# Warm-up matmuls that read a constant of the preamble, begun without VectorE, and two more of them

## Chip, cores, metric

One core of a Trainium2 chip. The metric is device microseconds of the whole kernel, the median over runs.

## The reference

The output mixes two branches of the same input x of 2048 tokens by 1024, both gated by a sigmoid. Branch a, a diagonal complex state-space model with 1024 states, is nearly all of the work at the start:

```python
g = sigmoid((x * gate_w).sum(-1, keepdims=True))
Bu = einsum("bld,pd->blp", x, B_bar)          # real and imaginary planes
h  = Lam_bar * h + Bu[:, t, :]                # scan over t
a  = 2.0 * einsum("blp,dp->bld", hseq, Cmat).real + x * Dskip
b  = x + scatter(moe(x[top 8 tokens]))
out = g * a + (1 - g) * b
```

## The kernel before

What the change and the argument touch is the first 24 us. The sync queue issues, one behind the other, the transposing loads of B (two planes, eight blocks) and of x; PE warms its clock with 14 matmuls on a zeroed tile, transposes the first 256 rows of x, which are loaded plainly, and starts on B.

```python
for tl in range(BPC):                                   # x rows 0..255, plain loads
    (nc.scalar if tl else nc.sync).dma_start(x0r[:, tl, :], x2d[tl * P:(tl + 1) * P, :])
load_B(0, 0, 1)                                         # transposing loads on the sync queue
...
new_X(0)
load_xT(1)                                              # x rows 256..511, transposing load
load_B(1, 0, 1)
for c0, c1 in ((1, 2), (2, 3), (3, 4), (4, 6), (6, 8)):
    for pl in range(2):
        load_B(pl, c0, c1)
...
wt0 = small.tile([P, LC], BF16, name="wt0", tag="wt")
nc.vector.memset(wt0[:], 0.0)
...
def warm(n):
    for _ in range(n):
        nc.tensor.matmul(wps[:], lhsT=wt0[:, 0:P], rhs=wt0[:], start=True, stop=True)

warm(14)
for tl in range(BPC):
    xq = ps_s2.tile([P, KD, P], BF16, name="xq", tag="zps")
    for dc in range(KD):
        nc.tensor.transpose(xq[:, dc, :], x0r[:, tl, dc * P:(dc + 1) * P], ident[:])
    ...                                                 # VectorE and ScalarE copy xq into X[0]
warm(2)
...
warm(1)
s1u(0, 0, 0, 0, 1)       # 8 matmuls, block 0 of B, real plane, first half of x
warm(2)
s1u(0, 0, 0, 1, 2)       # second half
s1u(0, 0, 1, 0, 2)       # imaginary plane
...
M["xsel32"] = small.tile([P, KD, 32], BF16, name="xsel32", tag="wt")   # reuses wt0's buffer
nc.gpsimd.memset(M["xsel32"][:], 0.0)
```

The results of the warm-ups are read by nobody.

## Time and profile before

| | |
|---|---|
| median, 3 runs | 247.49 us (247.28 to 247.5) |
| profiled execution | 247.9 us, span 246.1 us |
| first warm-up | 1.07 us |
| x0r lands, transposes begin | 4.11 us |
| PE's last wait for a load of B ends | 23.61 us |
| PE's last matmul ends | 242.95 us |

The lines of the profile stand in the prediction. Read them in this order: the chain, to see who sets the end in which stretch; the waits of PE; then the timeline of the stretch that the change touches. In a line of the timeline the columns are start, length of the group, engine, line, operation, names and shapes, count, and in brackets the idle time before it with its releaser. A group's length is from its first start to its last end, and the end of a matmul is modelled, so step times are worked out from starts.

### The profile page before, as it was taken

The numbers are of one execution on the slowest core, as the hardware profiler recorded it, in microseconds if no ns is written. First come the engines' busy times: TensorE is split into PE (matmuls) and PEld (weight loads), VectorE is DVE, ScalarE is ACT, GpSimd is POOL, SyncE is SP. The second block draws the span as 40 slices with busy tenths as digits, with TensorE's granted clock in tenths as the row PEclk, the third lists the DMA queues.
The fourth block names the chain that finished last, engine by engine and source line by source line (L and its number), as shares of the span: only waits on it lengthen the run. The fifth ranks groups of instructions, "written<-read, shape, count | busy, mean of one in ns | idle before, by whom it ended". The sixth has DMA issues, their size and how long they took to land.

```text
span 246.1 us, 3533 instructions
## 1 busy us (share of the span) xinstructions
PE 240.6 (98%) x1381; PEld 112.2 (46%) x1381; DVE 226.2 (92%) x230; ACT 119.3 (48%) x206; POOL 26.8 (11%) x47
## 2 busy tenths in 40 slices
PE   8998999999999999999999999999999999999994
PEld 5443444444444444444444444444444444446453
DVE  1799999999999999999999999999999999999932
ACT  3699973333462572223355462235267445456421
POOL 4000000000000301620002040100100211110210
PEclk9999999999999999999999999999999999999999
DMA  7899999999760450666257979778599999962052
GB/s 195 194 149 226 230 244 273 202 239 284 236 181 0 106 153 0 134 125 224 77 188 218 351 226 338 237 224 314 184 390 286 363 306 296 89 142 37 3 133 82
DMA packets 65313, 48.48 MB, mean 197 GB/s; under 512 B 50560, under 2 KB 52224, under 8 KB 65296
## 3 DMA queue, kind: packets, MB, share of 16 engines
q1 hardware_dynamic: 59968, 37.20, 58.1%
q0 software_dynamic: 3264, 7.38, 14.3%
q10 hardware_dynamic: 2064, 3.68, 4.1%
q8 instruction: 11, 0.18, 0.3%
q14 instruction: 6, 0.05, 0.1%
HBM read 27.55 MB, written 8.40 MB: 146 GB/s over the span
## 4 chain that ended last, share of the span: by engine, by line
PE 89%; SPq 7%; DMA 2%; issue 0%; DVE 0%
PE zps L767 42%; PE vps L271 39%; SPq L80 6%; PE zps L783 3%; PE pgu L659 3%; DMA BT<-in_A_B_im_dram 2%; PE y L671 1%; SPq L92 1%; PE zr L485 1%; DVE ot L788 0%; SPq L77 0%; PE xselT_ps L572 0%; PE zs_ps L588 0%; PE zt L492 0%; PE fl_ps L535 0%
## 5 line engine op out<-in xcount | busy, mean ns | idle before, releaser
L271 PE MATMUL vps<-X,BT 128*128 128x512 bf16 (+1 forms) x520 | 112.6, 376 | 1.2 <-DMA BT<-in_A_B_im_dram 0.9
L767 PE MATMUL zps<-CT,H 128*128 128x512 bf16 x480 | 105.0, 379 | 0.0
L271 PEld LDWEIGHTS <-BT 128*128 128x128 bf16 x520 | 50.1, 98 | 61.7 <-DMA BT<-in_A_B_im_dram 1.7
L767 PEld LDWEIGHTS <-H 128*128 128x128 bf16 x480 | 46.5, 98 | 56.6 <-issue 1.3
L278 ACT CAST V<-vps 128x512 bf16<-128x512 f32 x64 | 34.3, 588 | 58.6 <-PE vps L271 58.6
L308 DVE TENSOR_TENSOR_SCAN U<-d,U 128x2048 bf16<-128x2048 f32 (+2 forms) x22 | 62.0, 2860 | 0.6
L772 ACT ACTIVATE ot<-zps,gcol 128x512 bf16<-128x512 f32 x30 | 20.6, 686 | 46.3 <-PE zps L767 46.3
L741 ACT CAST zps<-xd 128x512 f32<-128x512 bf16 (+1 forms) x29 | 16.6, 576 | 3.6 <-ACT xt L728 3.3
L297 DVE TENSOR_TENSOR U<-V,T2tab 128x4096 bf16<-128x4096 bf16 (+2 forms) x11 | 16.6, 1511 | 0.7 <-ACT V L278 0.2
L298 DVE TENSOR_TENSOR V<-V,nTi 128x4096 bf16<-128x4096 bf16 (+2 forms) x11 | 16.7, 1516 | 0.5
L299 DVE TENSOR_TENSOR U<-U,V 128x4096 bf16<-128x4096 bf16 (+2 forms) x11 | 16.7, 1516 | 0.4
L793 POOL DMA_DIRECT2D out_dram<-ot x14 | 12.9, 923 | 32.5 <-ACT ot L772 30.4
L333 DVE TENSOR_TENSOR U<-U,S2tab 128x4096 bf16<-128x4096 bf16 x7 | 16.0, 2292 | 0.2
L335 DVE TENSOR_TENSOR H<-H,U 128x4096 bf16<-128x4096 bf16 x7 | 16.0, 2292 | 0.2
L728 ACT ACTIVATE xt<-xt,omgcol 128x1024 bf16<-128x1024 bf16 x14 | 16.0, 1144 | 0.0
L331 DVE TENSOR_TENSOR H<-U,Ctab 128x4096 bf16<-128x4096 bf16 x7 | 16.0, 2284 | 0.0
L705 POOL DMA_DIRECT2D xt<-in_A_x_dram x12 | 7.1, 594 | 80.9 <-DMA out_dram<-xt 42.9
L366 DVE TENSOR_TENSOR_SCAN U<-D,U 128x1024 bf16<-128x1024 f32 x4 | 8.9, 2279 | 0.1
L723 DVE TENSOR_TENSOR xd<-xt,Dbc 128x1024 bf16<-128x1024 bf16 x14 | 9.0, 683 | 0.0
L659 PE MATMUL pgu<-wgu,xsel 128*32 128x448 bf16 x128 | 7.2, 355 | 0.0
L783 PE MATMUL zps<-CT,H 128*128 128x256 bf16 (+1 forms) x48 | 7.1, 308 | 0.0
L718 POOL DMA_DIRECT2D out_dram<-xt x2 | 1.5, 752 | 49.2 <-DVE xt L717 49.2
(152 smaller groups left out, 127.6 us busy)
## 6 DMA issues: line engine op xcount, KB each, us to landing
wgu<-in_B_w_gate_dram SPq DMA_DIRECT2D x16, 448.0 KB, 3.5
wgu<-in_B_w_up_dram SPq DMA_DIRECT2D x16, 448.0 KB, 6.1
out_dram<-ot POOLq DMA_DIRECT2D x14, 256.0 KB, 6.0
wdb<-in_B_w_down_dram SPq DMA_DIRECT2D x7, 512.0 KB, 10.6
xt<-in_A_x_dram POOLq DMA_DIRECT2D x12, 256.0 KB, 4.3
out_dram<-xt ACTq DMA_DIRECT2D x12, 256.0 KB, 5.2
wd<-in_B_w_down_dram SPq DMA_DIRECT2D x5, 512.0 KB, 7.8
xt<-in_A_x_dram SPq DMA_DIRECT2D x4, 256.0 KB, 4.1
```

Of the source, the lines that this page charges most:

```text
L271: nc.tensor.matmul(o, lhsT=BT[pl][:, dc, ct * P:(ct + 1) * P], rhs=X[m][:, dc, k0 * LC:k1 * LC], start=(dc == 0), stop=(dc == KD - 1))
L278: nc.scalar.copy(out=V[k][:, :, ct, :], in_=vp[m, ct][:, :, kk, :])
L297: nc.vector.tensor_tensor(out=u, in0=v, in1=T2tab[:, :, c0:c1, :], op=ALU.mult)
L298: nc.vector.tensor_tensor(out=v, in0=v, in1=bc(nTi, c0, c1), op=ALU.mult)
L299: nc.vector.tensor_tensor(out=u, in0=u, in1=V[k][:, ::-1, c0:c1, :], op=ALU.add)
L308: nc.vector.tensor_tensor_scan(out=fl, data0=d0[:, c0:c1, :].rearrange("p c t -> p (c t)"), data1=fl, initial=0.0, op0=ALU.mult, op1=ALU.add)
L331: nc.vector.tensor_tensor(out=h, in0=g, in1=bc(Ctab, c0, c1), op=ALU.mult)
L333: nc.vector.tensor_tensor(out=g, in0=g, in1=S2tab[:, :, c0:c1, :], op=ALU.mult)
L335: nc.vector.tensor_tensor(out=h, in0=h, in1=G[k][:, ::-1, c0:c1, :], op=ALU.add)
L741: nc.scalar.copy(out=z[:], in_=xd[b][:, d_:d_ + w])
L767: nc.tensor.matmul(zps[:], lhsT=H[k][:, pl, ct, tl * P:(tl + 1) * P], rhs=CT[pl][:, ct, dsl], start=(fresh and ct == 0 and pl == 0), stop= ...
L772: nc.scalar.activation(out=ots[b][:, dsl], in_=zps[:], func=ACT.Copy, scale=gcol[:, b:b + 1])
```

## The change

The intent is to start the warm-ups without waiting for VectorE. They now read a constant of ones that the preamble writes before the barrier: one element per partition, read with a step of 0 as a 128x256 operand. Two more fill the time gained.

```diff
-    wt0 = small.tile([P, LC], BF16, name="wt0", tag="wt")
-    nc.vector.memset(wt0[:], 0.0)
+    wt0 = nc.const_aps.tensor(1.0, [P, LC], BF16)
...
-            nc.tensor.matmul(wps[:], lhsT=wt0[:, 0:P], rhs=wt0[:], start=True, stop=True)
-
-    warm(14)
+            nc.tensor.matmul(wps[:], lhsT=wt0[:, 0:P], rhs=wt0, start=True, stop=True)
+
+    warm(16)
```

## The prediction

> **What bounds the kernel now.** I read the page first (busy time, slices, chain), then the chain in order of time, then the waits of PE, then the timeline of the first microseconds, and last the busy time of chosen stretches.
>
> ```profile
> span 246.1 us, 3533 instructions
> PE 240.6 (98%) x1381; PEld 112.2 (46%) x1381; DVE 226.2 (92%) x230; ACT 119.3 (48%) x206; POOL 26.8 (11%) x47
> PE 89%; SPq 7%; DMA 2%; issue 0%; DVE 0%
> ```
>
> PE is busy 240.6 of 246.1 us, so idle 5.5 us in all. The chain that sets the end lies on PE for 89%, but 7% and 2% are the sync queue and a DMA. Where those 9% lie matters, since the change touches only the start. The chain in order of time:
>
> ```profile
> 0.74 0.39 SPq L77
> 1.20 1.32 SPq L80
> 2.57 2.60 SPq L92
> 5.21 1.31 SPq L80
> ...
> 14.68 3.56 SPq L80
> 18.24 0.04 issue
> 18.29 5.27 DMA BT<-in_A_B_im_dram
> 23.56 0.05 issue
> 23.61 36.43 PE vps L271 x168
> ```
>
> The first 23.6 us of the chain are not PE at all. They are a queue of transposing loads of B and x issued one behind the other by SP, each some 1.3 us or more, and the landing of a block of B_im at 23.56. PE takes the chain at 23.61 and keeps it. The waits of PE over the whole execution agree:
>
> ```profile
> PE wps L152 <- DVE halfpi L132: 1.1, 1, 1.1
> PE vps L271 <- DMA BT<-in_A_B_im_dram: 0.9, 2, 0.7
> PE vps L271 <- DMA X<-in_A_x_dram: 0.2, 1, 0.2
> ```
>
> PE waits 1.1 us for VectorE at the very start (the wait that the change takes away), and later 1.1 us for DMAs, of which 0.7 us is the wait that ends at 23.61. Then nothing. The busy times of four stretches (columns: stretch and length, then busy us and starts of PE, PEld, DVE, ACT, POOL, granted clock, DMA share, GB/s):
>
> ```profile
> 1.06:3.86 2.80, 2.79 (x14) 1.95 (x14) 0.00 (x0) 1.28 (x1) 2.17 (x7) 1.00 0.73 213
> 4.11:5.00 0.89, 0.89 (x17) 0.89 (x17) 0.23 (x1) 0.00 (x0) 0.00 (x0) 1.00 1.22 259
> 22.90:23.61 0.71, 0.00 (x1) 0.01 (x1) 0.71 (x3) 0.71 (x2) 0.00 (x0) 1.00 0.62 81
> 23.61:242.95 219.34, 219.30 (x1261) 101.02 (x1261) 208.91 (x181) 101.86 (x173) 23.61 (x32) 1.00 0.75 200
> ```
>
> From 23.61 to 242.95 PE is busy 219.30 of 219.34 us. Just before, from 22.90, it stands still for 0.71 us. So anything that PE does before 22.9 us is separated from the end by an idle stretch that a DMA ends. And the start itself:
>
> ```profile
> 0.84 0.17 DVE L129 MEMSET wt<- 128x128 uint32 x1 [0.84 <-PEq L932]
> 1.06 2.69 PEld L152 LDWEIGHTS <-wt 128*128 128x128 bf16 x14 [1.06 <-DVE halfpi L132]
> 1.07 3.06 PE L152 MATMUL wps<-wt 128*128 128x256 bf16 x14 [1.07 <-DVE halfpi L132]
> 4.11 0.90 PEld L159 LDWEIGHTS <-x0r 128*128 128x128 bf16 x16 [0.35 <-DMA x0r<-in_A_x_dram]
> 4.11 1.07 PE L159 MATMUL xq<-ident,x0r 128*128 128x128 bf16 x16
> 7.26 0.32 POOL L505 MEMSET xsel<- 128x256 bf16 x1 [4.04 <-PE wps L152]
> ```
>
> The 14 warm-ups begin at 1.07, after the memset (0.84 + 0.17 = 1.01, plus some 0.05 for the semaphore). Fourteen start within 1.06 to 3.86, the last about 3.86, so 13 steps in 2.79 us: 0.215 us each. The first useful work, the 16 transposes of x, begins at 4.11 because the load of x0r lands then, not because of the warm-ups.
>
> **What the Trainium skill says.** "TensorE: Matmul & The Clock Gate", Part 1, says that PE starts throttled at 1.2 GHz and goes to 2.4 GHz after some 3.4 us of sustained activity, seen through a window that runs freely and doesn't reset with the kernel; the gap of matmuls is N/1.2 ns cold and N/2.4 + 2.5 ns warm. For N = 256 that is 213 and 109 ns. The trace agrees: 215 ns a step for the warm-ups, while 17 starts (16 transposes of 128 columns and one warm-up) fit in 0.89 us from 4.11, or 52 ns each against the page's 56. So the switch came between about 3.86 and 4.11, some 2.8 to 3.05 us after PE's first matmul. (The granted clock of 1.00 in every stretch doesn't show this switch; the steps do.) "VectorE: DVE Perf Modes", section on zero memsets as uint32, says that a zero memset over 16-bit elements may run as uint32 at half the elements; the trace agrees: the 128x256 bf16 tile is written as 128x128 uint32 in 0.17 us. So what is removed was already cheap. The "FWL" row of the clock page's weight-path section allows column steps from -1,023 to 1,024, which includes the step 0 of the new operand; no run of before shows a step of 0.
>
> **The change part by part.**
> 1. The memset of wt goes: one VectorE instruction, 0.17 us at 0.84. VectorE has nothing else until the copy of X at 4.77 (it waits 3.75 us for PE there), so nothing on it moves: gain 0.
> 2. The first warm-up waits only for the start barrier. Other engines leave it at 0.74 (SP, POOL), 0.75 (ACT) and 0.84 (VectorE). I put PE's first matmul at 0.85, choosing the late end, so 1.07 - 0.85 = 0.22 us earlier.
> 3. Two more warm-ups at 0.215 cold: +0.43 us of PE, or +0.22 if both are warm (109 ns). If all 16 are cold the last step ends at 0.85 + 16 x 0.215 = 4.29. If the clock switches at about 3.95 as before, some 14.4 are done cold by then and the other 1.6 take 0.17: end about 4.12. If the switch moves with the start, to 3.73, 13.4 are done and 2.6 take 0.28: end about 4.01.
> 4. So the transposes begin at 4.11 to 4.29, against 4.11: between 0 and +0.18 us on PE there, and the first copies of X as much later. PE's slack behind: it waits 0.24 us for B_re at 5.93, 0.24 for x at 7.44, 0.18 for B_im at 8.65, and 0.71 before 23.61. The last two alone are 0.89 us. A delay of 0.18 disappears in the first of them; a gain disappears just as well, because the DMAs decide.
> 5. The sync queue: its transposing loads up to 23 us wait for earlier DMAs, and none for PE. The loads begin after the barrier at 0.74 and don't move: 0. The comparison of the two orders shows the sync and scalar queues with the same instructions and waits.
> 6. The clear of xsel on POOL reused the buffer of wt and waited 4.04 us for the last warm-up. In the new order it waits for nothing, so it goes after POOL's last DMA issue (2.66 + 0.56 = 3.22) instead of 7.26. POOL's next work is at 14.17: 0.
> 7. Four more PE rows (two weight loads, two matmuls), 0.43 us more busy time for PE, in a stretch before the bound begins.
>
> Sum on the path that sets the end: 0 + 0 + 0 = 0. Median 247.4 us, the 247.49 of before less a tenth for nothing but rounding: I expect no change.
>
> **The rivals.**
> (a) The earlier start is a real gain of 0.2 us, or more, because the clock switches earlier. For it: the authors evidently meant it, and 1.1 us is the longest wait of PE in the list. Against it: the transposes before are already at 52 ns a step, so warm when they begin, and x0r lands at 4.11 whatever PE does. It could pay only in executions in which the free window switches late (up to the page's 3.4 us later, half of it lost: 1.7 us, an estimate from the page, of which 0.9 us or more is absorbed). The three times, 247.28 to 247.5, show no such scatter. At best 246.7.
> (b) The two extra warm-ups replace the wait by work and delay the transposes by 0.18 us. For it: 16 x 0.215 = 3.44 us is longer than 4.11 - 0.85 = 3.26. Against it mattering: the 0.71 us idle before 23.61. It makes 247.5. Nothing of it reaches the end unless the scalar or vector work that hangs on X passes it on; after 23.61 PE shows no wait for them.
> (c) Reading one element over and over (step 0) is slower for PE. If each cold warm-up took twice as long, 16 x 0.43 = 6.9 us would end at 7.7, 3.6 us late; less the slack of 0.24 + 0.24 + 0.18 + 0.71 = 1.4 us, the end would come some 2.2 us later: 249.7. Still within 2%. Nothing in the trace speaks for or against; I give it 4%.
>
> **Range and chances.** The core is 0 +/- 0.2 us from the parts, the scatter of before is 0.22 us over three runs, and another chip or session may shift both by a few tenths. Range 246.9 to 247.9. To be faster by 2% would take 4.9 us, and PE's whole idle time is 5.5 us with 3.15 of it behind the last matmul: below 1%. Slower by 2% needs more than rival (c) gives: 1%. Within 2%: 98.5%.
>
> **What would show it right or wrong.** Right: the first warm-up at 0.75 to 0.9 waiting for no VectorE; 16 warm-ups with steps near 215 ns; transposes at 4.1 to 4.3; the clear of xsel near 3.2; the same SP issues at the same times; the DMA wait before 23.6 still there, shorter or longer by at most 0.2 us; PE from there to the end unchanged at about 219.3 us. Wrong: warm-up steps well above 215 ns, transposes beyond 5 us, or a wait before 23.6 that has vanished while PE begins that stretch later; a vanished wait together with an earlier landing of B_im would mean a gain that I don't see.

## The result

| | median | range | runs |
|---|---|---|---|
| before | 247.50 us | 247.19 to 247.58 | 6 |
| changed | 247.63 us | 247.31 to 248.19 | 6 |

The ratio is 1.0009, with a 95% interval of 0.9994 to 1.0024: no difference. Ratios in this document are the mean time of one kernel's runs over the mean of the other's runs of the same rounds. This one uses all six runs of each; those of the experiments come out, within 0.0002, when the first run of each list, the profiled one, is left out. So they are not quite the ratios of the medians quoted, which include it. Executions over 1.5% slower than the fastest of the same kernel are left out of the means.

The page of the changed kernel (span, and the chain by engine):

```profile
span 245.6 us, 3535 instructions
PE 98%; DVE 0%; issue 0%
```

The chain in order of time:

```profile
0.78 3.57 PE wps L151 x16
4.35 1.73 PE xq L158 x16
...
10.76 48.70 PE vps L270 x224
```

The timeline of the start and the only wait of PE in the whole execution:

```profile
0.78 3.57 PE L151 MATMUL wps<-const-bfloat16-1.0 128*128 128x256 bf16 x16 [0.78 <-PEq L931]
3.21 0.33 POOL L504 MEMSET xsel<- 128x256 bf16 x1
4.18 1.62 PEld L158 LDWEIGHTS <-x0r 128*128 128x128 bf16 x16 [0.32 <-DMA x0r<-in_A_x_dram]
4.19 1.89 PE L158 MATMUL xq<-ident,x0r 128*128 128x128 bf16 x16
10.69 48.77 PE L270 MATMUL vps<-X,BT 128*128 128x512 bf16 x224
```
```profile
PE wps L151 <- PEq L931: 0.8, 1, 0.8
```

And the stretch that holds the last 1261 starts of PE (columns as in the prediction):

```profile
23.20:242.41 219.21, 219.13 (x1261) 100.96 (x1259) 209.95 (x185) 102.77 (x175) 23.62 (x32) 1.00 0.76 199
```

Three things are to be seen. The start did what was intended: 0.78 instead of 1.07, and PE no longer waits for VectorE. But the first weight load of the transposes still waits 0.32 us, for the load of x, until 4.18, where before it waited 0.35 us until 4.11: what PE does first of use begins no earlier. Two things differ from before that the edit doesn't explain at once. First, the 16 transposes take 1.89 us from first start to last end where before they took 1.07: they ran at half rate, so the clock switched only near 6 us, not near 4. Second, the DMA waits of PE are gone, and the chain now lies on PE from 0.78 us on: 98% instead of 89%. PE does the rest in the same time as before (219.13 us for 1261 starts, against 219.30). So this one execution had a later clock, earlier loads, and a span 0.5 us shorter, while the medians say that nothing changed. Both oddities needed a test: are they the change, or chance?

### The profile page after: what moved, and what is told of

Its sections match the earlier page's. It is cut to its first block, busy times and chain, and to the rows that moved or that the text cites. A ratio compares the mean times of both kernels' runs of the same rounds, so it can differ in the third digit from the quotient of the medians.

```text
span 245.6 us, 3535 instructions
## 1 busy us (share of the span) xinstructions
PE 241.5 (98%) x1383; PEld 113.4 (46%) x1383; DVE 225.8 (92%) x229; ACT 119.1 (49%) x206; POOL 26.8 (11%) x47
## 4 chain that ended last, share of the span: by engine, by line
PE 98%; DVE 0%; issue 0%
PE vps L270 45%; PE zps L766 42%; PE zps L782 3%; PE pgu L658 3%; PE wps L151 2%; PE y L670 1%; PE zr L484 1%; PE xq L158 1%; DVE ot L787 0%; PE xselT_ps L571 0%; PE zs_ps L587 0%; PE zt L491 0%; PE va_ps L165 0%; PE vb_ps L435 0%; PE fl_ps L534 0%
```

## The experiments

The theories. W: the clock's window runs freely, so the moment of the switch varies from execution to execution in both kernels, and PE has enough slack ahead of the B loads to hide it. O: the new operand wakes the clock later. S: the slack is about 1 us, and what exceeds it costs time one for one. N: the start of PE doesn't matter at all. All comparisons are with the kernel before in the same rounds (11 or 12 runs of it, 6 of each experiment).

### The two kernels again

No edit. The kernel before:

> The kernel before, unchanged, for a second profile and to see the scatter. Theory W (the clock's window runs freely, so the switch falls anywhere, whatever the operand): ratio 1.000 within 0.15%, and the 16 transposes of x may now be cold (1.7 us) as well as warm (0.9 us). Theory O (the new operand, ones read with a step of 0, wakes the clock later than zeros in memory do): the transposes are warm again, about 0.9 us from first start to last. On the load of B: PE's DMA wait near 23.6 us is 0.7 us if that is a habit, anything from 0 to 0.7 if it is the scatter of the transposing loads.

Measured: 247.75 us median (247.31 to 249.01), ratio 1.0009 (0.9984 to 1.0034). The kernel before against itself gives the very ratio of the change: this is what noise looks like here. Its timeline:

```profile
1.07 3.17 PE L152 MATMUL wps<-wt 128*128 128x256 bf16 x14 [1.07 <-DVE halfpi L132]
4.27 1.85 PE L159 MATMUL xq<-ident,x0r 128*128 128x128 bf16 x16
```

Zeros in memory, 14 warm-ups, and the transposes are cold all the same. The changed kernel:

> The changed kernel, unchanged, for a second profile. Theory W: ratio 1.000 to 1.001, transposes warm or cold by chance. Theory O: transposes cold again (1.7 us), the switch near 6 us. If the change costs something steady of its own, the ratio stays above 1.001 with an interval that leaves 1 out.

Measured: 247.48 us median (247.19 to 249.07), ratio 0.9994 (0.9967 to 1.0021).

```profile
0.78 3.57 PE L151 MATMUL wps<-const-bfloat16-1.0 128*128 128x256 bf16 x16 [0.78 <-PEq L931]
4.25 1.09 PE L158 MATMUL xq<-ident,x0r 128*128 128x128 bf16 x16
```

Here the constant operand precedes warm transposes. The two kernels have changed places: theory O falls, and nothing speaks against W. A third profile of the changed kernel was taken with the last experiment below:

> The changed kernel once more, on the chip of the version above, for a third profile and more runs: ratio 1.000 within 0.2%, transposes warm or cold by chance.

Measured: 248.21 us median (247.31 to 248.99) on a chip where the kernel before had 248.32, ratio 0.9987 (0.9958 to 1.0016).

```profile
4.20 1.13 PE L158 MATMUL xq<-ident,x0r 128*128 128x128 bf16 x16
9.78 1.90 PE L270 MATMUL vps<-X,BT 128*128 128x512 bf16 x8 [0.95 <-DMA BT<-in_A_B_im_dram]
24.60 36.43 PE L270 MATMUL vps<-X,BT 128*128 128x512 bf16 x168 [0.60 <-DMA BT<-in_A_B_im_dram]
```

This execution had an early clock, and was the slowest of the changed kernel's three profiled ones (span 247.1 us): PE waited 1.6 us for B. In this execution the early clock bought nothing, and the late loads go with a span 1.5 us longer than in the first profile of the change.

### Only the earlier start

```diff
-    warm(16)
+    warm(14)      # on the changed kernel
```

> Only the earlier start: the constant operand with 14 warm-ups, so PE is free at 0.78 + 14 x 0.215 = 3.8 us and waits for x until 4.1 to 4.2. Theory W and the prediction: ratio 1.000 within 0.15%, same as the full change. If the two extra warm-ups are what costs, this one is faster than the full change by some 0.1 us; if the operand costs, it is as slow as the full change and its transposes are cold.

Measured: 248.06 us median (247.37 to 248.87), ratio 1.0014 (0.9992 to 1.0037). Warm transposes:

```profile
4.19 1.07 PE L158 MATMUL xq<-ident,x0r 128*128 128x128 bf16 x16 [0.37 <-DMA x0r<-in_A_x_dram]
```

Without the two extra warm-ups PE stands idle for 0.37 us until x lands, at the same 4.19 as with them. The interval holds 1, so this doesn't show a cost or a gain; it isn't faster than the full change either.

### Only the two extra warm-ups

```diff
-    warm(14)
+    warm(16)      # on the kernel before, memset kept
```

> Only the two extra warm-ups: VectorE's memset kept, 16 warm-ups, cold end at 1.07 + 16 x 0.215 = 4.5 us, so the transposes start up to 0.4 us after x has landed. The prediction: the delay is absorbed by the waits for the B loads, ratio 1.000 to 1.001. If PE has no slack in most executions, it is slower by 0.2 to 0.4 us (ratio 1.001 to 1.0016). Theory O: transposes warm.

Measured: 247.59 us median (247.27 to 248.35), ratio 0.9997 (0.9977 to 1.0016).

```profile
4.25 1.48 PEld L159 LDWEIGHTS <-x0r 128*128 128x128 bf16 x16
4.45 1.46 PE L159 MATMUL xq<-ident,x0r 128*128 128x128 bf16 x16
```

Here, unlike in the two kernels, the warm-ups hold up the transposes: the weight load at 4.25 waits for no DMA, and the first transpose follows at 4.45, behind the last warm-up. The switch falls into them, yet block 1 of B begins at 10.57, no later than in the other profiles, and the kernel isn't measurably slower. That such a delay of 0.2 to 0.3 us is absorbed fits this but isn't settled by the times: the interval reaches to 1.0016, which is 0.4 us. (The expectation of theory O, warm transposes, missed here too.)

### No warm-ups in front, and twice as many

```diff
-    warm(16)
+    warm(0)       # nowarm, on the changed kernel
+    warm(32)      # warm32, on the changed kernel
```

> The changed kernel with none of the 16 warm-ups ahead of the transposes (the five later ones stay). PE begins at about 4.2 us when x has landed, on a cold clock, and the switch comes between 7 and 10.5 us (2.9 to 6.3 us after the first matmul, an estimate from the switches seen: near 4 and near 5.9 us with a first matmul near 0.8 to 1.1). The transposes take 1.7 us, and the following matmuls of the first blocks run at half rate until the switch: PE some 1.5 to 3 us later than now at 10.6 us. Theory S (PE's slack before the B loads is about 1 us, so warm-ups matter only beyond it): slower by 0.3 to 2 us, ratio 1.001 to 1.008. Theory N (the start of PE doesn't matter at all, the loads decide up to 23 us): ratio 1.000 within 0.15%, DMA wait near 23 us still there.

Measured: 248.27 us median (247.47 to 248.86), ratio 1.0025 (1.0004 to 1.0046): slower by about 0.6 us (0.0025 x 247.7), though this is near the noise: with every run counted, also the 249.59 us of the kernel before, the means differ by 0.45 us.

```profile
4.27 1.89 PE L158 MATMUL xq<-ident,x0r 128*128 128x128 bf16 x16 [4.27 <-DMA x0r<-in_A_x_dram]
11.34 48.83 PE L270 MATMUL vps<-X,BT 128*128 128x512 bf16 x224
```

> The changed kernel with 32 warm-ups in front, to measure the slack: they end at 5.9 us if the clock switches near 4 and at 6.7 us if near 5.9, so the transposes come 1.7 to 2.5 us after x has landed. Theory S: no DMA wait is left before 23 us and the kernel is slower by 0.4 to 1.4 us, ratio 1.0015 to 1.0055. Theory N: ratio 1.000 within 0.15%.

Measured: 248.79 us median (248.01 to 249.47), ratio 1.0037 (1.0014 to 1.0061): slower by about 0.9 us.

```profile
6.94 1.05 PE L158 MATMUL xq<-ident,x0r 128*128 128x128 bf16 x16
12.65 48.76 PE L270 MATMUL vps<-X,BT 128*128 128x512 bf16 x224
```

Theory N falls, on warm32 above all: the start of PE does matter once the delay is large enough. The two expectations were off in size: without warm-ups PE came to block 1 0.65 us later than in the first profile of the change (11.34 against 10.69), not 1.5 to 3 us, and 32 warm-ups put the transposes some 2.7 us behind the landing of x, not 1.7 to 2.5. In the profile of 32 warm-ups the run of block 1 begins at 12.65 instead of 10.69 us, and the gate matmuls 1.96 us later than in the first profile of the change: in this profile the delay goes through whole once the slack is used up. The transposes began 2.75 us late (6.94 against 4.19) but ran 0.84 us faster, warm instead of cold, which leaves the 1.9 us that arrived at block 1 and at the gate matmuls. The first profile of the change had no wait left to absorb any of it: its cold transposes had used up the slack. The six runs fall into two groups, 248.01 to 248.31 and 249.26 to 249.47, and the profiled one is in the upper (249.29), with the clock switching near 6.2. An early switch would end 32 warm-ups about 1 us sooner; that this makes the lower group is consistent with W but wasn't profiled.

### Against the wait for B: single-block loads

```diff
-    for c0, c1 in ((1, 2), (2, 3), (3, 4), (4, 6), (6, 8)):
+    for c0, c1 in ((1, 2), (2, 3), (3, 4), (4, 5), (5, 6), (6, 7), (7, 8)):
```

On the changed kernel (split) and on the kernel before (splitb).

> The changed kernel with the loads of the last four blocks of B in single blocks, so that the first of them lands earlier. If the wait of PE near 23 us (0.2 to 0.7 us where the profiles show one) is due to the two-block loads, it goes, and the scatter with it: median 0.1 to 0.4 us lower, ratio 0.998 to 1.000. If the rate of the loads as such is what PE waits for, or PE has no wait in most executions, ratio 1.000 within 0.15%.

> The kernel before with the same single-block loads. If the earlier warm-up has a value that the late B loads hide, the changed kernel with single loads is faster than this one by 0.1 us or more. The prediction's view: no difference between the two within the interval, as x lands after the warm-ups in both.

Measured: split 247.7 us median (247.19 to 249.19), ratio 1.0005 (0.9979 to 1.0032); splitb 247.92 us median (247.28 to 248.85), ratio 1.0013 (0.9992 to 1.0035). The hoped-for gain didn't come. The wait near 23 us is gone in both profiles, as it is in five of the nine with unsplit loads, so the edit can't be credited with it; and both have a wait at 9.1 us:

```profile
9.12 1.90 PE L271 MATMUL vps<-X,BT 128*128 128x512 bf16 x8 [0.53 <-DMA BT<-in_A_B_im_dram]
```

(This line is of splitb.) It ends on the imaginary plane of block 0, ahead of everything that the edit touches, so it is taken for scatter of the loads, and it may hide what the edit gained. Between the two versions the medians differ by 0.2 us, inside both intervals: no value of the earlier start shows here either.

### A version that goes for the loads: x by PE

If the loads set the pace, take one off the queue: rows 256 to 511 of x, too, are loaded plainly (scalar queue) and transposed on PE.

```diff
-    x0r = const.tile([P, BPC, D], BF16, name="x0r", tag="XP2")
+    x0r = const.tile([P, 2 * BPC, D], BF16, name="x0r", tag="XP2")
...
+    for tl in range(BPC, 2 * BPC):
+        nc.scalar.dma_start(x0r[:, tl, :], x2d[tl * P:(tl + 1) * P, :])
...
-    load_xT(1)
...      # after rdec: the same transposes and copies for tl = 2, 3
-    s1u(0, 0, 0, 0, 1)
-    warm(2)
-    s1u(0, 0, 0, 1, 2)
+    s1u(0, 0, 0, 0, 2)
```

> A version that goes for what the start waits for: the second half of the first x block (rows 256 to 511) is no longer loaded by a transposing DMA (2.5 to 3.0 us of the sync queue ahead of the B loads in all profiles) but plainly on the scalar queue and transposed on PE, 16 more transposes. The B loads are issued some 2.6 us earlier. If the B loads set the pace of the start, the DMA waits of PE at 8.6 and 23 us go and the first two-block run begins 0.2 to 0.8 us earlier than 10.6 us: median 0.2 to 0.8 us lower than before, ratio 0.997 to 0.999. If the 0.9 us of transposes and their copies cost as much as the waits did, ratio 1.000 within 0.15%. A landing of x rows 256 to 511 after 6.5 us would make it slower.

Measured: 251.28 us median (249.41 to 253.79), ratio 1.0119 (1.0073 to 1.0166): slower by 1.2%. This isn't all due to the start. Its run of 253.79 us is in the median, not in the ratio, and four of its six runs have a mean granted clock of 0.985 to 0.993, where no other run here is below 0.997. The two at a clock of 1.000 took 249.41 and 249.51 us, about 1.1 us more than the mean of the kernel before (248.33). So about 1.1 us is what the profile, one of these two, can explain; why the clock was lower in the others was not found.

```profile
6.75 0.62 PE L159 MATMUL xq<-ident,x0r 128*128 128x128 bf16 x8 [1.14 <-DMA x0r<-in_A_x_dram]
8.24 0.62 PE L159 MATMUL xq<-ident,x0r 128*128 128x128 bf16 x8 [0.88 <-DMA x0r<-in_A_x_dram]
9.38 3.61 PE L276 MATMUL vps<-X,BT 128*128 128x512 bf16 x16 [0.41 <-DVE X L162]
13.06 48.52 PE L276 MATMUL vps<-X,BT 128*128 128x512 bf16 x224
```

The last case named in the expectation came true: the extra x rows were issued at 2.49 and 4.14 us and landed at 6.7 and 8.2, and the second DVE copy had to follow. The run of block 1 begins at 13.06. Moving a load to another queue didn't make it come sooner. Part of this is the issue: the second of the two loads left the scalar queue 1.65 us after the first. The rest is the landing: some 4.1 us after the issue, against 3.3 to 3.6 us for the first x rows in the kernel before. That it competes with the transposing loads of B, now issued earlier, for the same DMA engines fits this, but no run isolates it. No version run here beats the two kernels.

### The profiles side by side

Nine of the twelve profiles; split, splitb and x1pe, whose loads differ, are left out. From the timelines: length of the 16 transposes, start of the run of block 1 of B, PE's waits for B (blocks of the B loads only), start of the gate matmuls, span, all in us. The switch shows in the steps: 0.213 us cold and 0.109 to 0.114 warm for a warm-up, 0.107 and 0.056 for a transpose. The packed traces (trace.npz) also hold the granted clock's own record of it, which prof doesn't list; the column is from there, in us after PE's first matmul, and the steps agree within 0.2 us. mem16 has no such record: its figure is from the steps.

| run | switch after | transposes | block 1 | waits for B | gate | span |
|---|---|---|---|---|---|---|
| before | 2.8 | 1.07 | 10.62 | 0.9 | 59.97 | 246.1 |
| before again | 4.9 | 1.85 | 10.86 | 0 | 59.84 | 246.0 |
| mem16 | about 4.3 | 1.46 | 10.57 | 0 | 59.38 | 245.6 |
| changed | 5.2 | 1.89 | 10.69 | 0 | 59.39 | 245.6 |
| changed again | 3.6 | 1.09 | 10.61 | 0.4 | 59.44 | 246.5 |
| changed, third | 3.3 | 1.13 | 11.74 | 1.6 | 60.97 | 247.1 |
| const14 | 2.8 | 1.07 | 10.61 | 0.6 | 59.60 | 245.8 |
| nowarm | 3.7 | 1.89 | 11.34 | 0 | 60.10 | 246.3 |
| warm32 | 5.5 | 1.05 | 12.65 | 0 | 61.35 | 247.5 |

With 14 or 16 warm-ups in front (the first seven rows): where the clock switches late, PE arrives at block 1 at 10.57 to 10.86 without waiting; where it switches early, it arrives at 10.61 after waiting (or later, when the load is late). From the gate matmuls to the end all but one take 186.1 to 186.2 us (changed again: 187.1, of which 0.5 is a wait for a load of x). So nearly everything that differs is settled by the first 60 us, and there by the later of two: PE's own work, or the landing of B. The records of the clock say one thing more for W: in all eleven traces that have them the stretch at full clock lasts 70, 71 or 72 times 3.413 us (238.93, 242.35 or 245.76), whatever the kernel. That fits a window of fixed length that runs on by itself, with the first matmul at another place in it from execution to execution.

## Why the prediction was right, point by point

It said 247.4 us, no change; measured 247.63 us, ratio 1.0009. It gave two reasons: the transposes begin when x lands, and an idle stretch that a DMA ends, at 23.61, cuts the start off from the end. The first holds in every profile of the two kernels; the second in some executions only. Of its steps:

1. and 2. The memset moved nothing, and the first warm-up began at 0.78 (said: 0.85, chosen late). (VectorE did have something else early: the memset of halfpi at 0.96, which the step overlooks; it went to 0.81.)
3. The cold step was right: 0.213 us (said: 0.215), the longest warm-up in the profile of the change is 417 ns against 421 before, and 16 took 3.57 us with the modelled end of the last. The 52 ns for a warm transpose was a miscount: the x17 of that window includes a warm-up still in progress. The 16 steps from 4.11 to 5.01 are 56 ns each, just what the step expected of a warm one. The moment of the switch was wrong. The step took one of two moments, 3.95 or 3.73 us, from a single profile; the runs have it from 2.8 to 5.5 us after the first matmul: 2.8 and 4.9 in the two profiles of the kernel before, 3.3, 3.6 and 5.2 in the three of the changed one. Its rival (a) had named the late switch, but took the three close times as a sign against it. They were none: executions with a late switch (before again, changed) are no longer than the others.
4. The transposes began at 4.19, within 4.11 to 4.29, and this is the step that carries the result: their first weight load waits for x until 4.11 and 4.26 in the two profiles of the kernel before, and until 4.18, 4.24 and 4.20 in the three of the changed one, and const14, with PE idle for 0.37 us, has 4.19 too. The start gained ends at the landing of x. That the copies of X come at most 0.18 us later was wrong: cold transposes cost 0.8 us more, and the first copy of X began at 5.26 instead of 4.77. The slack absorbed this too, as the step had added it up: the waits at 5.93, 7.44 and 8.65 had vanished, and block 1 began 0.07 us later. That slack absorbs a small delay fits mem16 within the noise; that it ends is shown by warm32 (2 us later at block 1, 0.9 us of cost on average), and nowarm agrees. The wait at 23.61 was no part of this: the second profile of the unchanged kernel has none, nor has the first of the changed one, and their spans (246.0 and 245.6 us) are no longer than the 246.1 of the profile with it.
5. The sync queue issued its first two loads at the same 0.74 and 1.20 us; later ones up to 23 us moved by up to 0.5 us because the loads' own durations scatter, not because of PE.
6. The clear of xsel moved to 3.21 (said: 3.22), to no effect.
7. PE's busy time rose by 0.9 us, 0.4 of it the two warm-ups and most of the rest the cold transposes, all ahead of the bound.

Rival (b) didn't show: begun at 0.78 and not at 0.85, the 16 warm-ups are done by about 4.15 even when all are cold (the last starts at 3.93 or 3.94), and x lands at 4.18 or later in the three profiles. Of the versions with 14 or 16 warm-ups only mem16, which keeps the late start, has this delay. Rival (c) is out: with a step of 0 in the operand a cold warm-up has the same step, 0.213 us. What would have shown the prediction wrong, a vanished wait near 23 us, did happen, with B landing earlier; the repeats show it as chance, since the changed kernel has the wait in its second (0.21 us) and third profile (0.60 us), and the kernel before lacks it in its second.

One thing the prediction had too small: the scatter. It took 0.22 us from three runs. The kernel before alone spans 247.17 to 249.59 over the later rounds, and on one chip its median was 248.32. The ratio held on all of them; the range of 246.9 to 247.9 held for the session of the result, not for that chip.

What stays open: no effect below some 0.2% can be told from noise here, so a gain or loss of some 0.5 us by the change is not excluded (its three comparisons, 1.0009, 0.9994 and 0.9987, lean to neither side); and why the first two-block load of B_im holds the sync queue for 2.07 us in one execution of the changed kernel and 4.25 in another was not found.

## What to carry to other kernels

Before shortening the start of an engine, look for the next thing that it waits for: here an earlier start of the warm-ups bought nothing, since the first data landed after them either way, and work hidden ahead of a wait is free in both directions until the slack is used up. A single profile fixes neither the clock's switch nor the landing of loads; take a second one of both kernels before explaining a difference that the times don't show. Here the 16 warm-ups in front were worth about half a microsecond of 247, so a start a quarter of a microsecond earlier could hardly have been seen.

## What the Trainium skill lacked or had wrong

- "TensorE: Matmul & The Clock Gate", Part 1, gives the switch as about 4 us into sustained activity, plus or minus 0.5, and a window of 3.4 us that runs freely. The window agrees (stretches at full clock of 70, 71 or 72 times 3.413 us), and so does its note that the count of cold matmuls varies from run to run; the 0.5 is too narrow: eleven traces have the switch 2.8 to 5.5 us after the first matmul. Three of them (before, const14, x1pe) have it at 2.8 us, less than one window, so a whole window of sustained activity, which the page's table asks for, wasn't needed. The page doesn't say whether the operand matters for the switch: warm-ups on one constant read with a step of 0 had the same cold step (0.213 us), nearly the same weight loads (medians of 147 to 152 ns against 151 to 152) and switches in the same range as those on a zeroed tile.
- The same page, Part 4, says that the full clock doesn't engage for transposes on PE and gives some 275 ns each in a kernel. Here sixteen 128x128 bf16 transposes were recorded with 219 ns each in a warm stretch and 314 ns in a cold one (their ends are modelled), in steps of 56 and 107 ns: they run at the full clock once it is granted. (The trace lists them as matmuls with the identity as one operand; whether the page's transpose mode is on in them it doesn't show.)
- "DMA: Bandwidth & Descriptors", section "DMA Transpose (X-bar)", has no figure for the scatter of a transposing load. The same load of x held the sync queue for 2.37 to 3.01 us, and the first two-block load of B_re for 2.30 to 3.73 us, from one profile to another.
